# Filler matmuls into a free PSUM bank, a later planned end for TensorE's results, and a new order, in a planned one-core kernel

## The chip, the cores and the metric

The kernel runs on one core of a Trainium2 chip. The metric is the device time of one execution in microseconds (us); the time of the kernel before is the median of 3 runs. Engines go by these names: PE or TensorE (matmuls), DVE or VectorE, ACT or ScalarE, POOL or GpSimd, SP or SyncE, on whose queue all DMAs of this kernel are issued.

## What is computed

The reference is a sliding-window attention (half of the heads with a plain window of 32 tokens, half with a dilated one of 32 tokens in steps of 4), whose output feeds a first MLP (softmax-gated, with a layer norm) and a second one (softplus).

```python
# q, k, v: (4, 8, 576, 64); scores masked per head, softmax, times v
x = attn_out.transpose(0, 2, 1, 3).reshape(2304, 512)
h = x @ w_in                                   # 512 -> 1024
e = exp(h - max(h)); solu = h * e / (sum(e) + 1e-9)
y = (solu - mean) / sqrt(var + 1e-6) * g_ln @ w_out   # 1024 -> 512
h2 = y @ w2_in                                 # 512 -> 2048
out = softplus(h2) @ w2_out                    # 2048 -> 512, (2304, 512)
```

## The kernel before

Nearly every product is computed in three matmuls of fp16 halves: each operand is split into a high half and a low half (high by high, high by low, low by high). So each weight block is loaded in fp64, converted to fp32 by three VectorE instructions (`to_f32`, L768), squared and summed on ScalarE for its scale, and split into the two halves (`weights`, L791). There are 48 such blocks: 8 of w_in, 8 of w_out, and four quarters of the second MLP with 4 + 4 blocks each (`w2_quarter`, L887).

The attention is done in 28 pairs of blocks. The first 10 run in fp32 (`pair32` and `block32`, L1040 and L1081), because their inputs' scales aren't known yet: TensorE transposes q and k into a bank, computes scores, transposes the exponentials and multiplies by v; the result is transposed into columns of a bank and copied into a ring `xr`, the high half by ScalarE or VectorE (L631 or L667, the helpers), the low half by VectorE (L643). The other 18 pairs run in fp16 halves with DMA transposes (`block`, L1184). The first MLP takes 18 tiles of 128 tokens (`m1`, L1287), its second matmul and the second MLP 9 groups of 256 tokens (`y_stage`, L1390, and `mlp2`, L1437).

PSUM has eight banks of 512 fp32 columns here: `banks[0]` to `banks[3]`, shared by the attention and by the outputs of y_stage and mlp2 (several pools with one flag `taken` per bank, L611 and L612), and two double banks `ps_w` for the wide results.

Nothing is issued in the order in which it is written. Each step is an `Op` with its possible engines and costs, its predecessors and its buffers. `Plan.order` (L148) then plays the execution through in Python: a clock, one ready list per engine sorted by due time (`TABLE`, one number in tenths of a microsecond for each of the 2524 steps), the costs `act_cost`, `dve_cost`, `pe_cost` (L280: duration, and time until others see the result) and `moving` (L288: a DMA's time on the queues). A buffer is free in the plan when the last user has ended there. The resulting order is emitted engine by engine and kept; the engines then run it in order and wait for each other with semaphores.

Where TensorE has nothing ready in the plan before 400 us, a filler of `FILL` = 0.24 us is planned (L261 to L265: `None` in the order). The emission (L1581 and after) turns it into a 512-column matmul of `eye` into the first `ps_w` as long as no step has used `ps_w`, and after that into eight matmuls of 60 columns into columns 452 to 511 of bank 1 (L1590), which no step reads. Bank 1 also holds attention results and small sums in its other columns.

Lines that the rows name: L631 ScalarE activation, L635 and L637 VectorE tensor-scalar, L640 VectorE scalar-tensor-tensor, L643 VectorE tensor-tensor, L646 reciprocal, L649 matmul, L655 TensorE transpose.

Of the kernel before, what the change touches and what calls it, by code (L numbers as in the profile page):

```python
# [24 lines left out]
class Pool:  # L25
# [8 lines left out]
    def add(self, t, until=10 ** 9, since=0, opens=(), place=None):  # L34


        self.slots.append([t, until, since, list(opens), [False] if place is None else place])
# [28 lines left out]
class Plan:  # L66
# [8 lines left out]
    FILL = (0.24, 0.48)  # L75
# [9 lines left out]
    def __init__(self, due, table):  # L85
        self.ops = []
        self.due, self.table = due, table

# [59 lines left out]
    def order(self):  # L148
# [25 lines left out]
        while events:  # L174
            now = heapq.heappop(events)
            while ends and ends[0][0] <= now + 1e-9:
                _, i, elsewhere = heapq.heappop(ends)
                o = self.ops[i]
                if elsewhere:
                    over.add(o)  # L180
                    for b in o.uses:
                        b.left -= 1
                        if b.left == 0:
                            b.slot[4][0] = False
                for s in o.succ:
                    for e in s.opts:
                        if (e != o.on) == elsewhere:
                            s.wait[e] -= 1
                            if not s.wait[e] and s.on is None:
                                bisect.insort(ready[e], (s.late + self.shy(s, e), s.i))  # L190
# [70 lines left out]
            if idle_at["PE"] <= now + 1e-9 and now < self.FILL_END:  # L261
# [3 lines left out]
                out.append(None)  # L265
# [14 lines left out]
def pe_cost(us):  # L280
    return {"PE": (us, 0.12)}
# [6 lines left out]
def moving(packets, size, lag=2.2):  # L288

    return 1.07 * packets * (12 + size / 21.0) / 16000, lag  # L290
# [3 lines left out]
def kernel(  # L294
# [1332 lines left out]
```

## Time and profile before

| | us |
|---|---|
| median of 3 runs | 722.39 (720.72 to 723.04) |
| profiled execution, own time | 724.25 |
| its span, first to last instruction | 722.40 |
| TensorE busy in the span | 695.0 (96%) |
| VectorE busy | 510.1 (71%) |
| ScalarE busy | 460.1 (64%) |

The profile counts an engine's busy time by instruction; a filler counts as busy like any matmul. A row with "x968" is a group of 968 instructions, then their busy time in us and the mean ns of one, from its start to its modelled end, so that matmuls that follow each other overlap. Behind it stands the idle time of the engine just before them, and what ended it ("<-"). "Waits" rows read: who waited, for whom, us in total, times, the longest. PEclk is the granted clock of TensorE as a share of 2.4 GHz.

### The profile page before, as it was taken

How to read it: one execution, taken by the hardware profiler on the slowest of the kernel's cores; microseconds unless marked ns; L12 is line 12 of the kernel's file. 1: busy time of each engine (PE TensorE's matmuls, PEld its weight loads, DVE VectorE, ACT ScalarE, POOL GpSimd, SP SyncE). 2: the span in 40 equal slices, each digit the busy share in tenths (PEclk: the TensorE clock that was granted, in tenths of full speed). 3: DMA queues.
4: the chain of work that ended last, by engine and by line, in shares of the span. 5: the costliest groups of instructions: out<-in, count | busy, mean ns of one | idle time of the engine just before them, and what ended most of it. 6: DMA issues, size and time to landing. Idle time of an engine off the chain costs nothing.

```text
span 722.4 us, 15990 instructions
## 1 busy us (share of the span) xinstructions
PE 695.0 (96%) x6186; PEld 494.3 (68%) x6186; DVE 510.1 (71%) x1550; ACT 460.1 (64%) x938; POOL 3.5 (0%) x22
## 2 busy tenths in 40 slices
PE   6789889999999999999999999999999999999997
PEld 3566777868766577777665866776686567778573
DVE  4899889999999894966889578489857662310411
ACT  4687788698999486777785489268756552321121
POOL 1000000000000000000000000000000000000000
PEclk9879999999999999999999999999999999999999
DMA  9987866767875446976775185465614111100100
GB/s 250 297 216 216 232 155 155 173 147 159 188 181 143 127 135 171 233 129 156 154 127 111 45 179 128 74 110 127 127 37 74 41 30 27 33 1 1 59 1 29
DMA packets 186779, 89.91 MB, mean 124 GB/s; under 512 B 157000, under 2 KB 174416, under 8 KB 186704
## 3 DMA queue, kind: packets, MB, share of 16 engines
q1 hardware_dynamic: 186704, 88.90, 52.5%
q8 instruction: 48, 0.79, 0.5%
q14 instruction: 27, 0.22, 0.1%
HBM read 54.53 MB, written 4.72 MB: 82 GB/s over the span
## 4 chain that ended last, share of the span: by engine, by line
PE 77%; DVE 13%; DMA 5%; ACT 4%; issue 1%; SPq 0%; DVEq 0%; ACTq 0%
PE bank L649 39%; PE ps_w L649 32%; PE bank L1590 3%; DVE W L640 3%; DMA E<-in_moe_w_in_dram 2%; DMA W<-in_v_dram 1%; PE bank L655 1%; DVE E L640 1%; ACT xr L631 1%; DMA kT<-qk 1%; ACT E L631 1%; DVE xr L643 1%; ACT xf L631 1%; DMA xd<-x 1%; DVE s L1202 1%
## 5 line engine op out<-in xcount | busy, mean ns | idle before, releaser
L649 PEld LDWEIGHTS <-W 128*128 128x128 f16 x2592 | 252.0, 98 | 35.8 <-issue 0.4
L649 PE MATMUL bank<-y,W 128*128 128x256 f16 x1728 | 197.9, 273 | 0.3 <-DVE y L640 0.3
L649 PE MATMUL ps_w<-W,g 128*128 128x512 f16 x864 | 195.0, 379 | 0.0
L649 PEld LDWEIGHTS <-g 128*128 128x128 f16 x864 | 83.5, 98 | 90.9
L649 PE MATMUL ps_w<-W,xr 128*128 128x512 f16 x432 | 97.9, 379 | 0.0
L649 PE MATMUL bank<-lnT,W 128*128 128x256 f16 x864 | 97.4, 273 | 0.0
L631 ACT ACTIVATE r<-bank,invC 128x512 f32<-128x512 f32 x72 | 49.2, 685 | 71.9 <-PE bank L649 63.8
L640 DVE SCALAR_TENSOR_TENSOR g<-r,KR,g 128x512 f16<-128x512 f32 x72 | 53.6, 745 | 51.7 <-ACT g L631 48.9
L1595 ACT ACT_TABLE_LOAD x59 | 75.7, 1283 | 1.1
L649 PEld LDWEIGHTS <-xr 128*128 128x128 f16 x432 | 41.6, 99 | 44.9 <-issue 0.2
L631 ACT ACTIVATE s<-s 96x128 f32<-96x128 f32 (+3 forms) x144 | 43.7, 375 | 15.9 <-DVE s L637 15.7
L631 ACT ACTIVATE E<-E 128x768 f32<-128x768 f32 (+3 forms) x53 | 38.8, 733 | 9.7 <-DVE E L640 5.9
L1202 DVE CUSTOM_DVE_ANT_0 s<-bank,band,bsc 96x128 f32<-96x128 f32 (+3 forms) x144 | 39.0, 324 | 4.3 <-PE bank L649 3.7
L1590 PE MATMUL bank<-eye 128*128 128x60 bf16 x968 | 34.2, 191 | 7.7 <-DVE xr L643 2.5
L1590 PEld LDWEIGHTS <-eye 128*128 128x128 bf16 x968 | 31.9, 98 | 9.9 <-issue 9.4
L635 DVE TENSOR_SCALAR g<-r,KR 128x512 f16<-128x512 f32 x29 | 13.9, 478 | 35.1 <-PE ps_w L649 30.6
L640 DVE SCALAR_TENSOR_TENSOR y<-bank,y 128x512 f16<-128x512 f32 x18 | 12.3, 685 | 33.8 <-ACT y L631 33.8
L631 ACT ACTIVATE y<-bank 128x512 f16<-128x512 f32 x18 | 10.7, 592 | 37.7 <-PE bank L649 37.6
L631 ACT ACTIVATE g<-r,KR 128x512 f16<-128x512 f32 x43 | 30.8, 720 | 5.1 <-PE ps_w L649 4.2
L631 ACT ACTIVATE hl<-e,st 128x1024 f16<-128x1024 f32 x18 | 22.2, 1235 | 15.9 <-DVE st L640 9.7
L631 ACT ACTIVATE xf<-bank,rs 80x64 f32<-80x64 f32 (+1 forms) x104 | 23.6, 305 | 11.4 <-DVE rs L646 8.6
L631 ACT ACTIVATE e<-ps_w,st,bsc 128x1024 f32<-128x1024 f32 x16 | 19.3, 1204 | 13.8 <-DVE st L635 6.7
(190 smaller groups left out, 891.2 us busy)
## 6 DMA issues: line engine op xcount, KB each, us to landing
E<-in_moe_w_in_dram SPq DMA_DIRECT2D x19, 512.0 KB, 5.4
E<-in_moe_w_out_dram SPq DMA_DIRECT2D x16, 512.0 KB, 4.2
out_dram<-osb SPq DMA_DIRECT2D x18, 256.0 KB, 2.1
W<-in_moe_w_out_dram SPq DMA_DIRECT2D x8, 512.0 KB, 4.7
E<-in_q_dram SPq DMA_DIRECT2D x9, 384.0 KB, 3.4
E<-in_k_dram SPq DMA_DIRECT2D x9, 384.0 KB, 3.4
E<-in_v_dram SPq DMA_DIRECT2D x9, 384.0 KB, 3.3
W<-in_moe_w_in_dram SPq DMA_DIRECT2D x5, 512.0 KB, 8.9
```

What stands on the lines that cost most here:

```text
L631: pin(nc.scalar.activation(out=out, in_=in_, func=func, **kw))
L635: pin(nc.vector.tensor_scalar(out=out, in0=in0, scalar1=s1, scalar2=None, op0=op0))
L640: pin(nc.vector.scalar_tensor_tensor(out=out, in0=in0, scalar=s, in1=in1, op0=op0, op1=op1, **kw))
L643: pin(nc.vector.tensor_tensor(out=out, in0=a, in1=b, op=op))
L649: pin(nc.tensor.matmul(out, l, r, start=start, stop=stop))
L655: pin(nc.tensor.transpose(out, in_, eye32[:in_.shape[0], :in_.shape[0]]))
L1202: pin(nc.vector.tensor_tensor_reduce(out=sv()[:rows, h, :nk], in0=sb.t[:rows, h, :nk], in1=band[:rows, 48 - m:48 - m + nk], scale=sc[:rows ...
L1590: pin(nc.tensor.matmul(banks[1][:, 452:512], eye, eye[:, 0:60], start=False, stop=False, skip_group_check=True))
L1595: pin(nc.scalar.preload_act_table_set(TABLES[tab]))
```

## The change

Three things change.

- A filler goes into a bank that is free in the plan at that moment, the one that has been free longest: each bank's flag now holds the time at which it came free, `fills` lists the four banks and the first half of both `ps_w`, and the order holds the chosen bank in place of `None`. If none is free, `None` stays in the order and nothing is emitted, though the plan still counts the filler. It is always one matmul of 512 columns; the eight small ones, and the one before them, are gone. `FILL` goes from 0.24 to 0.235 us.
- The plan's numbers: a TensorE result is seen by others 0.26 us after its matmul (0.2 for long ones) where it was 0.12; a DMA takes 1.05 in place of 1.07 times its formula and 2.05 in place of 2.2 us of lag, unless a call names its own lag.
- `TABLE`, the due times of all steps, is replaced as a whole, so that the order is another.

```diff
-        self.slots.append([t, until, since, list(opens), [False] if place is None else place])
+        self.slots.append([t, until, since, list(opens), [False, 0.0] if place is None else place])
...
-    FILL = (0.24, 0.48)
+    FILL = (0.235, 0.48)
...
+        self.fills = []
...
                         if b.left == 0:
-                            b.slot[4][0] = False
+                            b.slot[4][:] = [False, now]
...
-                out.append(None)
+                free = [f for f in self.fills if not f[0][0]]
+                out.append(min(free, key=lambda f: f[0][1])[1] if free else None)
...
 def pe_cost(us):
-    return {"PE": (us, 0.12)}
+    return {"PE": (us, 0.26 if us < 2 else 0.2)}
...
-def moving(packets, size, lag=2.2):
+def moving(packets, size, lag=2.05):
 
-    return 1.07 * packets * (12 + size / 21.0) / 16000, lag
+    return 1.05 * packets * (12 + size / 21.0) / 16000, lag
...
     TABLE = (
-        132, 520, 330, 83, 561, 140, 146, 157, 191, 249, 235, 436, 342, 89, 150, 150, 164, 172, -3353, 168,
...
-    taken = [[False] for _ in banks]
+    taken = [[False, 0.0] for _ in banks]
...
+    P.fills = [*zip(taken, banks), *((x[4], x[0][:, 0]) for x in ps_w.slots)]
     order = P.order()
-    tab, unused = 1, True
-    mm(banks[1][:, 452:512], eye, eye[:, 0:60], True, True)
+    tab = 1
     for o in order:
         if o is None:
-            if unused:
-                mm(ps_w.slots[0][0][:, 0], eye, eye.unsqueeze(1).broadcast_to([128, 4, 128]), True, True)
-                continue
-            for _ in range(8):
-                pin(nc.tensor.matmul(banks[1][:, 452:512], eye, eye[:, 0:60], start=False, stop=False, skip_group_check=True))
             continue
-        unused = unused and not any(b.pool is ps_w for b in o.uses)
+        if not isinstance(o, Op):
+            mm(o, eye, eye.unsqueeze(1).broadcast_to([128, 4, 128]), True, True)
+            continue
```

## Rows read from the trace of the kernel before

**Rows 1.** The page, busy time of each engine over the span.

```profile
PE 695.0 (96%) x6186; PEld 494.3 (68%) x6186; DVE 510.1 (71%) x1550; ACT 460.1 (64%) x938; POOL 3.5 (0%) x22
```

**Rows 2.** Busy time by stretch: length, engines, granted clock, DMA share, GB/s.

```profile
core 0: us, PE busy (x) PEld busy (x) DVE busy (x) ACT busy (x) POOL busy (x), PEclk, DMA share, GB/s
0.00:40.00 40.00, 30.41 (x201) 20.20 (x201) 26.80 (x73) 23.27 (x68) 3.52 (x22) 0.83 1.00 270
40.00:160.00 120.00, 109.73 (x1532) 84.25 (x1531) 109.79 (x317) 96.11 (x257) 0.00 (x0) 0.97 0.71 184
160.00:255.00 95.00, 92.84 (x829) 64.58 (x828) 92.31 (x278) 79.68 (x168) 0.00 (x0) 1.00 0.67 160
255.00:718.00 463.00, 461.98 (x3630) 325.28 (x3627) 280.49 (x886) 260.35 (x447) 0.00 (x0) 1.00 0.42 89
```

**Rows 3.** The fillers of L1590 alone, by stretch: length, PE and PEld busy, clock, DMA.

```profile
40.00:160.00 120.00, 30.12 (x848) 28.06 (x848) 0.97 0.71 184
160.00:255.00 95.00, 4.11 (x120) 3.81 (x120) 1.00 0.67 160
sum 722.40, PE 34.23 PEld 31.87; mean PE 6.85 PEld 6.37
```

**Rows 4.** TensorE's groups of instructions, shapes apart: fillers, and a matmul of 512 columns.

```profile
L649 PE MATMUL ps_w<-W,g 128*128 128x512 f16 x864 | 195.0, 379 | 0.0
...
L1590 PE MATMUL bank<-eye 128*128 128x60 bf16 x968 | 34.2, 191 | 7.7 <-DVE xr L643 2.5 <-ACT xf L631 2.3 <-ACT xr L631 1.7
L649 PE MATMUL ps_w<-eye 128*128 128x512 bf16 x40 | 14.1, 469 | 0.0
```

**Rows 5.** Timeline of 103 to 111 us: start us, us, instruction, idle before it.

```profile
103.82 0.33 ACT L631 ACTIVATE xr<-bank 128x192 f16<-128x192 f32 x1 [0.37 <-PE bank L1590]
...
104.21 0.38 PE L1590 MATMUL bank<-eye 128*128 128x60 bf16 x8 [0.42 <-ACT xr L631]
...
105.20 0.36 DVE L643 TENSOR_TENSOR xr<-bank,xr 128x192 f16<-128x192 f32 x1 [1.31 <-PE bank L1590]
```

**Rows 6.** VectorE's waits from 40 to 160 us.

```profile
DVE xr L643 <- PE bank L1590: 4.1, 5, 1.3
DVE tmp L819 <- PE bank L1590: 1.6, 3, 0.6
DVE xr L643 <- ACT xf L631: 0.9, 1, 0.9
DVE rs L637 <- PE bank L649: 0.9, 2, 0.7
DVE rs L637 <- ACT xf L631: 0.7, 1, 0.7
DVE pT L667 <- PE bank L655: 0.3, 1, 0.3
DVE W L637 <- DMA E<-in_moe_w_in_dram: 0.3, 1, 0.3
...
DVE rs L637 <- PE bank L1590: 0.2, 1, 0.2
```

**Rows 7.** ScalarE's waits for TensorE from 40 to 160 us.

```profile
ACT xr L631 <- PE bank L655: 3.8, 3, 1.5
...
ACT xr L631 <- PE bank L1590: 1.9, 3, 1.1
...
ACT qT L631 <- PE bank L649: 1.3, 1, 1.3
...
ACT xf L631 <- PE bank L1590: 0.5, 1, 0.5
```

**Rows 8.** TensorE's timeline from 84 us, ten groups of eight fillers in a row.

```profile
84.35 2.36 PE L1590 MATMUL bank<-eye 128*128 128x60 bf16 x80 [0.58 <-ACT xr L631]
```

**Rows 9.** The chain of work, 40 to 130 us: start us, us, what.

```profile
92.33 2.59 PE ps_w L649 x12
```

**Rows 10.** The page's DMA issues: count, KB each, median us to landing.

```profile
E<-in_moe_w_in_dram SPq DMA_DIRECT2D x19, 512.0 KB, 5.4
```

286 rows, old and new, of the table TABLE are left out of this document.

## The prediction

> **What bounds the kernel now.** I read the page's busy shares first. TensorE is busy 96% of the span [rows 1], which invites the conclusion that only fewer matmuls could help. The table by stretch and the rows of the fillers correct that. From 255 to 718 us TensorE is idle for 463.00 - 461.98 = 1.0 us, without a filler: a solid block of work that no order can shorten, and behind it lie 4.4 us for the last copy and its store. Before 255 us it is idle for 9.6, 10.3 and 2.2 us in the three stretches [rows 2], and 34.2 us of its "busy" time are fillers of 60 columns at L1590 [rows 3], 14.1 us more the early fillers of 512 columns [rows 4]. So 22.1 + 48.3 = 70 us of the span are TensorE waiting for others. The rest is work that stays. The span falls only if the block starts earlier, hence only if whoever feeds TensorE before 255 us gets faster.
>
> Who feeds it? From 40 to 160 us VectorE is busy 109.8 of 120 us, ScalarE 96.1; from 160 to 255 us VectorE 92.3 of 95 us, ScalarE 79.7 [rows 2]. VectorE converts the weights, writes the low halves into the ring xr and takes the maxima, so VectorE's lost time sets the pace until TensorE is saturated. In 40 to 160 us it lost 10.2 us.
>
> **Where VectorE loses it.** The timeline at 104 us shows the mechanism. ScalarE writes the high half of xr out of a bank (103.82 to 104.15). The next filler starts only at 104.21, after 0.42 us of idling, and names ScalarE's xr as its releaser. VectorE's xr, which reads the same bank after ScalarE, starts at 105.20, after 1.31 us of waiting for a filler [rows 5]. Fillers and readers both use bank 1 and take turns, although the filler's columns 452 to 511 are never read. From 40 to 160 us VectorE waits for fillers 4.1 + 1.6 + 0.2 = 5.9 us [rows 6] and ScalarE 1.9 + 0.5 = 2.4 us [rows 7]; TensorE idles 7.7 us ahead of fillers in the whole execution [rows 4].
>
> **The change part by part.**
>
> *Fillers into a free bank.* A group of eight 60-column matmuls becomes one of 512 columns. Ten groups in a row took 2.36 us [rows 8], 0.236 us a group; twelve 512-column matmuls of the real work took 2.59 us [rows 9], 0.216 each. For 121 groups that is 2.4 us less of filler, which costs or brings nothing: fillers stand where TensorE has nothing else. A real matmul can now be late by at most one 0.216 us filler, before by a group of 0.236. What does count is the bank. The new filler takes the one that has been free longest by the plan, so each reader of the old contents has finished by the plan, and a later reader waits only for the real matmul between. VectorE's 5.9 us go. I take all of them as gain, because VectorE has no slack there that could have covered them. ScalarE's 2.4 us I take as nothing: its 24 us of idle time there cover them; without the cover they would be the further end, 8.3 us. The lower end is nothing, if other waits step in. The fillers' own 7.7 us I also put at nothing, hidden behind VectorE.
>
> Which wait is a bank's and which an address's? The rows show two operations on different columns of one bank waiting for each other. The Trainium skill, "PSUM — Partial Sum Buffer", section "PSUM bank collisions raise a hardware error", asks that accesses be guarded by bank and quadrant, not by address, which agrees with that row; by its rule a whole-bank filler in a bank that is still being read would also wait, which is the rival "not free" below.
>
> *TensorE's results planned later.* The plan allowed 0.12 us from a matmul's slot to its consumer, now 0.26 or 0.20. A 512-column matmul's mean row is 0.379 us [rows 4] for a 0.216 us slot, so 0.16 us pass before its end: 0.12 was too little, and engines that work in order were given consumers of TensorE that weren't ready. What that costs now: VectorE waits for real matmuls 0.9 + 0.3 = 1.2 us in 40 to 160 us [rows 6], ScalarE 3.8 + 1.3 = 5.1 us [rows 7]. I take VectorE's whole and a quarter of ScalarE's, since it has 24 us idle: 1.2 + 1.3 = 2.5 us. Ends: 0 and 6.3 us.
>
> *Loads planned earlier.* 1.07 to 1.05 and 2.2 to 2.05 us put a load's planned arrival earlier by 0.15 us and 2% of the queue's backlog: 0.15 + 0.02 x 40 = at most 0.95 us after the first 40 us, where the DMA share is 1.00 [rows 2]. VectorE waits for loads 0.3 us in 40 to 160 us [rows 6], so there is spare time: nothing taken, the other end is the slower rival.
>
> *The order made anew.* Nearly all of the table's 2524 due times are new; what each moves on the queues can't be read from the profile of before. Bounds: the one stretch with TensorE dry behind a saturated VectorE is 160 to 255 us, 2.2 us idle and 4.1 us of fillers [rows 2, 3], so 6.3 us could go; for a loss I take the same size. I take 0, because VectorE, nearly full there, leaves an order little to win. Each step of the work still runs once, on the same queues, with the same 48 weight blocks to load.
>
> *The first matmul of 60 columns* goes away: one filler less while VectorE still waits for its first weights; nothing.
>
> **Sum.** 5.9 + 2.5 = 8.4 us. The profiled execution took 724.25 us, 722.40 of them the span and 1.85 around it, which I leave. That run lies 1.86 us above the median of 722.39 us, so I take the 8.4 us off the median: **714.0 us**. With its own ends this case spans 709 (most of what ScalarE waits for fillers and late matmuls, 2.4 and the other 3.8 us, is gained as well: 5 us more) to 719 (the replanning gives nothing, and the order loses 2.5).
>
> **The rivals.**
>
> *The dry stretch closes too* (0.20): the 6.3 us of 160 to 255 us go as well, 722.4 - 8.4 - 6.3 = 707.7 us. For it: with VectorE 8 us ahead, the last quarter's weights are ready when TensorE's stock runs out. Against: VectorE is as full there as before.
>
> *VectorE's time is given back* (0.14): after 160 us TensorE and VectorE are both above 97% [rows 2], and a VectorE that is ahead meets other waits, such as ScalarE's share of the same chains (xf, 0.9 + 0.7 us [rows 6]). Then about 1 us stays, 721.4 us. Against it: that stretch has no wait of any size on VectorE today.
>
> *The banks aren't free* (0.07): the change doesn't do what it says, if on the chip the readers lag behind the plan and fillers still wait. The 5.9 us stay lost and the 2.5 come, 719.9 us. Against: the bank is the longest free.
>
> *VectorE stuck behind a load* (0.10, slower): VectorE works in order; if a conversion is put ahead of its load's arrival, everything behind it waits. The place is 20 to 160 us, with the 40 blocks after the first eight, each landing some 5.4 us after its issue [rows 10]. The price is up to 0.95 us each by the sum above; the point is (8.4 + 2.2)/40 = 0.27 us per block, from which the run is slower than before. At 0.4 us each: 714 + 16 = 730 us. For it: the DMA share of 1.00 early. Against: 0.3 us of such waits in 40 to 160 us.
>
> *A clock that falls* (0.03): where no bank is free by the plan, nothing is emitted, where before a filler always was. The granted clock was 0.83 in 0 to 40 us and 0.97 in 40 to 160 us with 30.1 us of small fillers [rows 2, 3]. At 0.83 the 109.7 - 30.1 = 79.6 us of real work there would take 79.6 x 0.97/0.83 = 93.0 us, 13.4 more, against 40 us of idle time and fillers. Half hidden: 714 + 6.7 = 720.7 us. The Trainium skill, "TensorE: Matmul & The Clock Gate", section "Why this matters for your kernels", warns of idle gaps between matmul bursts, after which the clock is halved; that speaks against leaving fillers out.
>
> **How the numbers follow.** 0.46 is left for the forecast. 0.3%, about what a measurement here tells from no change, is 2.2 us. Faster: 0.46 + 0.20 + 0.03 of the given-back case + 0.04 of the banks + 0.01 of the clock = 0.74. Same: 0.09 + 0.03 + 0.02 = 0.14. Slower: 0.02 + 0.10 = 0.12. The range 706 to 722 leaves out the load rival (0.10), half of the given-back case (0.07) and a little below the dry-stretch rival (0.03).
>
> **What would show it.** Right: no VectorE or ScalarE wait names the filler's line, VectorE's idle time in 40 to 160 us falls from 10.2 to about 4 us, fillers are of 512 columns and spread over several banks, TensorE's solid block starts some 8 us earlier and lasts as long, and the clock there is still near 0.97. Wrong: waits of TensorE's fillers for readers of their bank remain; VectorE waits for weight loads after 20 us; or the block starts earlier but has holes after 255 us, where each microsecond idle counts in full.

## The result and the profile after

The kernel after takes **714.1 us** (median of 4 runs, 713.2 to 715.53) where before takes 722.12 us in the same comparison (4 runs, 720.72 to 723.04): a ratio of 0.9892, 95% interval 0.9869 to 0.9916. That is 8.0 us less. The profiled execution took 715.53 us, the slowest of its four.

The page of the kernel after, its span and busy shares, which answer to [rows 1]:

```profile
span 713.8 us, 14287 instructions
...
PE 690.8 (97%) x5334; PEld 475.8 (67%) x5334; DVE 505.4 (71%) x1548; ACT 453.7 (64%) x913; POOL 3.5 (0%) x22
```

Busy time by stretch in the kernel after (length, PE, PEld, DVE, ACT, POOL with counts, granted clock, DMA share, GB/s), which answers to [rows 2]:

```profile
0.00:40.00 40.00, 34.11 (x244) 20.39 (x245) 27.06 (x70) 21.44 (x64) 3.52 (x22) 0.96 1.01 271
40.00:160.00 120.00, 110.70 (x815) 74.48 (x814) 115.09 (x336) 105.32 (x279) 0.00 (x0) 0.91 0.71 188
160.00:255.00 95.00, 93.12 (x717) 62.12 (x715) 91.31 (x286) 78.70 (x165) 0.00 (x0) 1.00 0.73 162
255.00:709.40 454.40, 452.84 (x3564) 318.82 (x3563) 271.20 (x859) 247.81 (x408) 0.00 (x0) 1.00 0.42 89
```

VectorE now loses 120 - 115.09 = 4.9 us from 40 to 160 us, before 10.2. Its waits there, which answer to [rows 6] (who, for whom: us, times, longest):

```profile
DVE xr L644 <- ACT xr L632: 1.6, 2, 1.3
DVE s L1094 <- PE bank L650: 1.6, 1, 1.6
DVE E L638 <- DMA W<-in_moe_w_out_dram: 1.0, 1, 1.0
DVE hl L644 <- ACT hl L632: 0.3, 1, 0.3
```

A filler and a real matmul now share line L650, so the one wait for TensorE needs a second look: `s` reads the bank in which scores were just computed, 1.6 us. The order of after with the old fillers, whose late ones have a line of their own, has the same wait of 1.6 us, and there it names the real matmuls' line. The waits of `xr` and `tmp` for TensorE that made up 5.7 of the 5.9 us in [rows 6] are gone. TensorE's fillers, which answer to [rows 3, 4]:

```profile
L650 PE MATMUL ps_w<-eye 128*128 128x512 bf16 x91 | 24.8, 392 | 0.6 <-DVE e L641 0.6
L650 PE MATMUL bank<-eye 128*128 128x512 bf16 x66 | 19.4, 423 | 4.0 <-POOL eye L709 4.0
```

There are 157 fillers of 512 columns, spread over single and double banks. The plan has 191: for 34 of the 76 that come after the first use of `ps_w` it finds no free bank, and nothing is emitted. Ahead of them TensorE idles 4.6 us, 4.0 of them before `eye` exists at the start. The 0.6 us that are left stand against the 7.7 us ahead of the small fillers before.

Where the 8 us went is a sum over TensorE, whose real work is the same in both kernels (695.0 - 48.3 = 646.7 and 690.8 - 44.2 = 646.6 us). Its time without real work (fillers, plus span minus busy) was 48.3 + (722.4 - 695.0) = 75.7 us before and is 44.2 + (713.8 - 690.8) = 67.2 us after. The difference of 8.5 us is the difference of the two spans, 8.6.

### The profile page after: what moved, and what is told of

Read it like the earlier page. It is cut to its first block, busy times and chain, and to the rows that moved or that the text cites. A ratio compares the mean times of both kernels' runs of the same rounds, so it can differ in the third digit from the quotient of the medians.

```text
span 713.8 us, 14287 instructions
## 1 busy us (share of the span) xinstructions
PE 690.8 (97%) x5334; PEld 475.8 (67%) x5334; DVE 505.4 (71%) x1548; ACT 453.7 (64%) x913; POOL 3.5 (0%) x22
## 4 chain that ended last, share of the span: by engine, by line
PE 70%; DVE 14%; DMA 8%; ACT 4%; issue 3%; SPq 0%; ACTq 0%; DVEq 0%
PE bank L650 38%; PE ps_w L650 30%; DVE W L641 2%; DMA pT<-p 2%; DMA E<-in_v_dram 1%; PE bank L656 1%; DMA rq<-in_q_dram 1%; DVE E L641 1%; DVE s L1203 1%; DVE e L641 1%; DMA W<-in_moe_w_out_dram 1%; DMA xr<-x 1%; DMA qT<-qk 1%; DMA xd<-in_v_dram 1%; DVE p L644 1%
## 5 line engine op out<-in xcount | busy, mean ns | idle before, releaser
L650 PEld LDWEIGHTS <-W 128*128 128x128 f16 x2592 | 252.2, 98 | 37.1 <-issue 2.0
L650 PE MATMUL bank<-y,W 128*128 128x256 f16 x1728 | 196.7, 273 | 1.0 <-ACT r L632 1.0
L650 PE MATMUL ps_w<-W,g 128*128 128x512 f16 x864 | 194.9, 379 | 1.0 <-DVE osb L641 1.0
L650 PEld LDWEIGHTS <-g 128*128 128x128 f16 x864 | 83.4, 98 | 92.6 <-issue 1.3
L650 PE MATMUL ps_w<-W,xr 128*128 128x512 f16 x432 | 99.7, 385 | 0.1
L650 PE MATMUL bank<-lnT,W 128*128 128x256 f16 x864 | 98.3, 273 | 0.3 <-DMA lnT<-hl 0.3
L650 PEld LDWEIGHTS <-xr 128*128 128x128 f16 x432 | 42.3, 100 | 48.1 <-issue 3.0
L632 ACT ACTIVATE E<-E 128x768 f32<-128x768 f32 (+3 forms) x56 | 40.4, 726 | 10.6 <-DMA E<-in_v_dram 3.2
L636 DVE TENSOR_SCALAR g<-r,KR 128x512 f16<-128x512 f32 x34 | 16.4, 482 | 37.1 <-PE ps_w L650 35.7
L632 ACT ACTIVATE y<-bank 128x512 f16<-128x512 f32 x15 | 8.9, 594 | 41.5 <-PE bank L650 41.5
L632 ACT ACTIVATE g<-r,KR 128x512 f16<-128x512 f32 x38 | 27.3, 719 | 5.5 <-PE ps_w L650 4.8
L650 PEld LDWEIGHTS <-eye 128*128 128x128 bf16 (+2 forms) x177 | 17.4, 106 | 19.6 <-issue 5.3
L1329 DVE TENSOR_REDUCE st<-ps_w 128x1 f32<-128x1024 f32 x18 | 21.9, 1216 | 7.0 <-PE ps_w L650 7.0
L641 DVE SCALAR_TENSOR_TENSOR E<-E 128x512 int32<-128x512 int32 x40 | 26.1, 683 | 0.0
```

Of the source, the lines that this page charges most:

```text
L632: pin(nc.scalar.activation(out=out, in_=in_, func=func, **kw))
L636: pin(nc.vector.tensor_scalar(out=out, in0=in0, scalar1=s1, scalar2=None, op0=op0))
L641: pin(nc.vector.scalar_tensor_tensor(out=out, in0=in0, scalar=s, in1=in1, op0=op0, op1=op1, **kw))
L650: pin(nc.tensor.matmul(out, l, r, start=start, stop=stop))
L1329: ({"DVE": (1.142, 0.14)}, lambda e: pin(nc.vector.tensor_reduce(out=col(0), in_=ph(), axis=AXX, op=ALU.max, negate=True)), [mb], [ps]),
```

## The experiments

Each kernel was timed against before on its own chip. Before's median was 722.59 us beside the fillers alone, the order alone, the early results and the old order with early fillers alone; 722.31 beside the small fillers in a free bank, the new order without late fillers and without any, and the first run with the bank freed last; 722.87 beside the other four. A difference between two kernels that ran on different chips is taken here from what each lost or won against its own before. "Old order" is that of before with its costs and table, "new order" that of after. The two crossed cases, the new table with all the old costs or the old table with all the new ones, give no complete order (the plan runs into a point where nothing can start), so they weren't tried. Medians in us, with the ratio to before and its interval:

| fillers | old order | new order |
|---|---|---|
| none | 724.29, 1.0015 (1.0000 to 1.0031) | 720.78, 0.9973 (0.9953 to 0.9993) |
| early ones alone | 722.4, 1.0001 (0.9987 to 1.0014) | 714.64, 0.9890 (0.9866 to 0.9914) |
| early, then 8 x 60 columns in bank 1 | before | 714.84, 0.9890 (0.9867 to 0.9913) |
| early, then 8 x 60 columns in a free bank | 716.1, 0.9907 (0.9883 to 0.9932) | not run |
| 512 columns, bank free longest | 714.9, 0.9887 (0.9870 to 0.9905) | after: 714.1, again 714.39, 0.9883 (0.9863 to 0.9902) |
| 512 columns, bank freed last | 715.23, 0.9903 (0.9883 to 0.9924) | 711.22, 0.9838 (0.9812 to 0.9864); again 710.96, 0.9842 (0.9821 to 0.9863) |

"Early" are those before a step uses `ps_w`: 40 in the old order, 115 in the new one.

**The fillers alone, in the old order.** Before, with the change's lists of free banks and its emission, but before's table, costs and `FILL`:

```diff
-                out.append(None)
+                free = [f for f in self.fills if not f[0][0]]
+                out.append(min(free, key=lambda f: f[0][1])[1] if free else None)
...
-            for _ in range(8):
-                pin(nc.tensor.matmul(banks[1][:, 452:512], eye, eye[:, 0:60], start=False, stop=False, skip_group_check=True))
...
+        if not isinstance(o, Op):
+            mm(o, eye, eye.unsqueeze(1).broadcast_to([128, 4, 128]), True, True)
+            continue
```

> The order of before, unchanged; only the fillers go, one matmul of 512 columns each, into the bank that the plan of before knows to be free. Bank theory: the 5.9 us that VectorE waited for fillers from 40 to 160 us go, and the time falls to about 716 us (714 to 718), ratio 0.992; no wait names a filler. Order theory: the fillers' waits only stood in place of other waits, the gain came from the new order, and this kernel takes 720 to 723 us, with VectorE's idle time from 40 to 160 us still near 10 us.

Measured: 714.9 us, 7.7 less than before. The same steps in the same order on each engine, and VectorE is busy 116.08 of 120 us. Its stretch from 40 to 160 us, then its longest waits there:

```profile
40.00:160.00 120.00, 113.34 (x842) 74.40 (x841) 116.08 (x330) 102.82 (x270) 0.00 (x0) 0.96 0.72 189
```

```profile
DVE s L1095 <- PE bank L651: 1.0, 1, 1.0
DVE tmp L821 <- PE bank L651: 0.9, 1, 0.9
DVE st L1330 <- PE ps_w L651: 0.4, 1, 0.4
DVE xr L645 <- ACT xr L633: 0.3, 1, 0.3
```

VectorE's idle time fell by 116.08 - 109.79 = 6.3 us, a little over the 5.9 of [rows 6]; no wait of `xr` for TensorE is left. Step by step against before, VectorE is level or up to 2 us behind until about 75 us, 4.2 us ahead at 111 us, 7.0 at 150 us, 6.5 at 200 us, 9.3 at its end (the profiled execution of before lies 1.9 us above its median, so part of the 9.3 is its own). So the lead is not given back. Of the 161 fillers that the plan has, 149 stand in this trace; for 12 it finds no free bank.

**The order alone, with the old fillers.** After, with before's fillers:

```diff
-                free = [f for f in self.fills if not f[0][0]]
-                out.append(min(free, key=lambda f: f[0][1])[1] if free else None)
+                out.append(None)
...
+            for _ in range(8):
+                pin(nc.tensor.matmul(banks[1][:, 452:512], eye, eye[:, 0:60], start=False, stop=False, skip_group_check=True))
```

> The order of the changed kernel with the fillers of before (eight of 60 columns in bank 1, and 512 columns in the first double bank until that is first used). Bank theory: VectorE waits some 5 us for fillers again, and the time rises from 714.1 to 718 to 721 us. Order theory: 714 to 715 us, no change from the changed kernel.

Measured: 714.84 us, as much as the fillers alone brought. The parts give 7.7 and 7.8 us, and together 8.0. They don't add: VectorE's idle time from 40 to 160 us falls from 10.2 us to 3.9 with the fillers alone, 4.5 with the order alone and 4.9 with both. The stretch, then TensorE's groups, whose late fillers still sit in bank 1:

```profile
40.00:160.00 120.00, 115.34 (x1323) 84.86 (x1323) 115.47 (x335) 105.32 (x276) 0.00 (x0) 0.96 0.69 189
```

```profile
L649 PE MATMUL ps_w<-eye 128*128 128x512 bf16 x115 | 32.2, 403 | 0.0
L1590 PE MATMUL bank<-eye 128*128 128x60 bf16 x608 | 21.1, 191 | 1.9 <-ACT xr L631 1.0 <-ACT xf L631 0.4 <-DVE rs L637 0.3
```

There are 608 / 8 = 76 groups in bank 1 where [rows 4] have 968 / 8 = 121, TensorE idles 1.9 us ahead of them instead of 7.7, and VectorE's waits for them in 40 to 160 us have one row:

```profile
DVE rs L637 <- PE bank L1590: 0.5, 1, 0.5
```

In the old order of instructions 40 late fillers stand between the high and the low half of a write of `xr`, in the new one 10. More of the filling (115 early ones where 40 were) happens while `ps_w` is still unused. So the new order's late fillers hold up little; where its gain comes from is told by the runs without them, below.

**Bank or size?** The fillers of the first experiment, but eight of 60 columns in place of one of 512 once `ps_w` is in use:

```diff
-    tab = 1
+    tab, unused = 1, True
...
-            mm(o, eye, eye.unsqueeze(1).broadcast_to([128, 4, 128]), True, True)
+            if unused:
+                mm(o, eye, eye.unsqueeze(1).broadcast_to([128, 4, 128]), True, True)
+                continue
+            for i in range(8):
+                pin(nc.tensor.matmul(o[:, 452:512], eye, eye[:, 0:60], start=i == 0, stop=True, skip_group_check=True))
             continue
+        unused = unused and not any(b.pool is ps_w for b in o.uses)
```

> The order of before; fillers go into the bank that the plan knows to be free, but the later ones stay eight matmuls of 60 columns each (columns 452 to 511 of that bank). If the bank is what counts, the time is that of the 512-column fillers in the free bank: 714 to 717 us, and no wait names a filler. If the size counts (one instruction for eight, fewer weight loads, shorter wait of real work behind a filler), it stays at 719 to 723 us.

Measured: 716.1 us, its interval overlapping that of the 512-column ones. It is the bank: against its own before this kernel wins 6.2 us, where the 512-column fillers won 7.7. The 1.5 us between them, which the intervals can't tell from nothing, are left for the size. Here the small fillers have a line of their own, L1594. TensorE idled before none of them, and no wait of VectorE or ScalarE before 260 us names that line:

```profile
L1594 PE MATMUL ps_w<-eye 128*128 128x60 bf16 x752 | 25.1, 191 | 0.0
...
L1594 PE MATMUL bank<-eye 128*128 128x60 bf16 x120 | 3.8, 190 | 0.0
```

**The late fillers taken away, old order.** Before without the loop of eight:

```diff
-            for _ in range(8):
-                pin(nc.tensor.matmul(banks[1][:, 452:512], eye, eye[:, 0:60], start=False, stop=False, skip_group_check=True))
```

> The kernel before without the eight-matmul fillers; the early ones of 512 columns stay. Bank theory: as with the free bank, VectorE's 5.9 us of waits for fillers go, but the clock is no longer held up in 60 to 160 us. If the clock hardly matters there because TensorE waits for VectorE anyway, 716 to 718 us; if the clock counts, the granted clock falls from 0.97 to about 0.8 from 40 to 160 us, and the time is 720 to 730 us.

Measured: 722.4 us, the same as before. Its stretch from 40 to 160 us and VectorE's longest waits in it:

```profile
40.00:160.00 120.00, 101.80 (x710) 68.78 (x711) 111.09 (x319) 97.68 (x257) 0.00 (x0) 0.84 0.70 183
```

```profile
DVE xr L667 <- PE bank L655: 1.6, 1, 1.6
DVE s L1093 <- PE bank L649: 1.4, 3, 0.6
DVE pT L667 <- PE bank L655: 1.3, 1, 1.3
DVE tmp L757 <- PE bank L649: 1.2, 1, 1.2
```

The waits for fillers are gone, and waits for real matmuls stand in their place: the granted clock there is 0.84, against 0.97 in [rows 2]. VectorE still loses 8.9 us. So before's 121 late groups were worth nothing net: what they held up in clock they took in waits. In a free bank the fillers (109 late ones) do only the first, 722.4 - 714.9 = 7.5 us.

**The same cuts in the new order, and no fillers at all.** First, after, whose fillers stop when a step uses `ps_w`:

```diff
-    tab = 1
+    tab, unused = 1, True
...
-            mm(o, eye, eye.unsqueeze(1).broadcast_to([128, 4, 128]), True, True)
+            if unused:
+                mm(o, eye, eye.unsqueeze(1).broadcast_to([128, 4, 128]), True, True)
             continue
+        unused = unused and not any(b.pool is ps_w for b in o.uses)
```

> The changed kernel without the fillers that come after the first use of a double bank; the early ones stay. If fillers pay by the clock also in the new order, as the old order without small fillers suggests (722.4 us with no filler to wait for), the granted clock from 40 to 160 us falls well below 0.91 and the time rises by 4 to 9 us, to 718 to 723 us. If the new order has little use for fillers, it stays at 714 to 716 us; that would also explain why the old fillers cost it nothing.

Then both orders without fillers: after's, and the first experiment's for the old order, each with this edit:

```diff
         if not isinstance(o, Op):
-            mm(o, eye, eye.unsqueeze(1).broadcast_to([128, 4, 128]), True, True)
             continue
```

> The changed kernel without any filler. If the early fillers, which hold the clock from 0 to 60 us, pay too, it is slower than the one without late fillers by some 2 to 8 us: 718 to 730 us. If VectorE sets the pace there whatever the clock, the same as without late fillers.

> The order of before without any filler. With the new order without any filler at 720.8 us, the difference is what the order alone is worth. If the order has a worth of its own of some 8 us, as with the old fillers, this takes 727 to 732 us. If its gain lay in where and how many fillers it places, 720 to 723 us.

Measured: 714.64, 720.78 and 724.29 us. The stretch from 40 to 160 us of the three, in that order:

```profile
40.00:160.00 120.00, 105.17 (x780) 72.16 (x779) 114.95 (x335) 104.97 (x276) 0.00 (x0) 0.90 0.69 189
```

```profile
40.00:160.00 120.00, 100.61 (x712) 70.65 (x711) 110.44 (x322) 98.75 (x269) 0.00 (x0) 0.82 0.69 182
```

```profile
40.00:160.00 120.00, 101.19 (x685) 68.90 (x684) 109.88 (x318) 96.21 (x259) 0.00 (x0) 0.83 0.72 184
```

In the new order the early fillers bring 720.78 - 714.64 = 6.1 us and the late ones nothing that can be told; the clock is 0.90 without the late ones and 0.91 with them. In the old order it is the other way round: the late ones in a free bank bring 7.5 us (0.84 to 0.96), the 40 early ones 1.6 (clock 0.83 and 0.84; 724.29 is 1.4 above its before, 722.4 is 0.2 below), and the intervals of those two kernels overlap. In these runs fillers pay where they raise the clock of that stretch and VectorE's idle time falls with it. The order by itself, without fillers, is worth 3.0 us (1.4 above its before in the old order, 1.5 below in the new one).

The two kernels with early fillers alone have no late filler that a reader could wait for, and the new order is still ahead, 7.7 us below its before against 0.2: 7.5 us. Of these 3.0 are the order's own, and 4.5 go with 115 early fillers in place of 40 (6.1 - 1.6). So the new order's gain with the old fillers does not come from turn-taking that it avoids. It comes without late fillers as well; the order only places them so that they cost little.

**Results planned early again.** After with the old time from a matmul to its consumer. The due times stay those made for 0.26 and 0.2:

```diff
-    return {"PE": (us, 0.26 if us < 2 else 0.2)}
+    return {"PE": (us, 0.12)}
```

> The changed kernel with TensorE's results planned at 0.12 us after their matmul, as before; the new due times and the new fillers stay, so the plan makes another order from the same due times. If the 0.26 and 0.20 us are worth what they save in waits for results that come later than planned, 2 to 3 us are lost: 716 to 718 us. If due times and costs only work as a pair that was searched for together, the order falls apart much further: over 722 us. If neither matters: 714 us.

Measured: 725.76 us, 1.0035 (1.0016 to 1.0055): 11.7 us over after, 3.2 us slower than before. But this is no measure of the term, because it changes the order as well, and the due times don't fit it. VectorE loses no more from 40 to 160 us (115.09 us busy); what is lost shows behind it, where ScalarE is busy 70.92 us in place of 78.70:

```profile
160.00:255.00 95.00, 93.12 (x692) 60.16 (x691) 91.08 (x278) 70.92 (x145) 0.00 (x0) 1.00 0.66 150
```

TensorE is as busy there as in after, but more of it is fillers. Its matmuls with `eye`, behind 160 us fillers only (length, busy, clock, DMA share, GB/s):

```profile
160.00:255.00 95.00, 9.13 (x37) 1.00 0.66 150
255.00:400.00 145.00, 4.26 (x19) 1.00 0.68 151
```

That is 13.4 us, where after has 2.4 us before 255 us and none behind it.

**The bank that was freed last.** If the plan's "free" were wrong on the chip, the bank freed last would bring the waits back. After, and the first experiment for the old order, with one word changed; and after once more, for its spread:

```diff
-                out.append(min(free, key=lambda f: f[0][1])[1] if free else None)
+                out.append(max(free, key=lambda f: f[0][1])[1] if free else None)
```

> The changed kernel with the filler in the bank that came free last by the plan, where it was the one that has been free longest. If the plan's free banks are free on the chip only because of that margin, fillers wait for readers again and the time rises by 2 to 6 us, to 716 to 720 us. If the plan is true to the chip within a few tenths of a microsecond, 714 to 715 us.

> The changed kernel once more, beside the one with the newest free bank. If that one is really faster, this takes 713 to 715 us again; if its 711.2 us were those of another chip, this takes about 711 us too.

> The changed kernel with fillers in the bank that came free last, once more. Really faster: 710 to 712 us, 2 to 4 us less than the changed kernel in the same job. A chip's difference: the same as the changed kernel.

> The order of before, 512-column fillers in the free bank that came free last by the plan. If the choice among the free banks matters by itself, this gains as in the new order, 2 to 4 us: 711 to 713 us. If the old order's plan, which takes TensorE's results 0.12 us after the matmul, is too early for a bank just freed, fillers wait for readers and it takes 716 to 720 us. If the choice doesn't matter: 715 us.

Measured: in the old order 715.23 us, the same as with the bank free longest (714.9). In the new order 711.22 and 710.96 us, below 714.1 and 714.39 for after, and each of its nine executions (709.72 to 712.29) lies below each of after's nine (712.51 to 715.53): this version **beats both kernels**, by 3.4 us against after in the last comparison. Its fillers do wait for others, but little: some 1.1 us in either order, without the 4.0 us for `eye` at the start. In the old order these waits are all ahead of one group:

```profile
L651 PE MATMUL bank<-eye 128*128 128x512 bf16 x73 | 20.2, 391 | 1.1 <-DVE xr L645 0.4 <-ACT xf L633 0.4 <-ACT kT L633 0.2
```

VectorE's instructions come in the same order with either bank. The profiled executions of the last comparison lie only 1.7 us apart (712.51, the fastest of its five, and 710.78), so they can show half of the difference at most. From 220 to 232 us the repeat of after stalls, here its row and then that of the version with the bank freed last:

```profile
220.00:232.00 12.00, 11.10 (x63) 5.35 (x62) 10.97 (x26) 8.16 (x18) 0.00 (x0) 1.00 0.68 132
```

```profile
220.00:232.00 12.00, 11.97 (x67) 5.74 (x66) 12.00 (x27) 8.93 (x18) 0.00 (x0) 1.00 0.73 129
```

VectorE loses 1.0 us there, because it waits for a ScalarE instruction that came after 3.26 us without a visible cause; in the first profile of after it came after 3.36 (timeline of the repeat of after, then of the other; start, us, instruction, idle before it):

```profile
225.88 0.63 ACT L632 ACTIVATE p<-s 96x512 f16<-96x512 f32 x1 [3.26 <-issue]
...
226.54 0.69 DVE L644 TENSOR_TENSOR p<-s,p 96x512 f16<-96x512 f32 x1 [1.03 <-ACT p L632]
```

```profile
224.18 0.63 ACT L632 ACTIVATE p<-s 96x512 f16<-96x512 f32 x1 [1.80 <-issue]
```

That can't be the whole cause: the version without late fillers has the short wait too (1.77 us) and takes 714.64 us. Why the other bank is 3.4 us faster in the new order, and not in the old one, **stays open**.

## Why the prediction was right, and which of its steps were not

The total came out: 714.0 us predicted, 714.1 measured, the 8.4 us taken off against 8.0. The split did not, so that the total is this close is partly luck.

**What bounds the kernel: right.** TensorE's 75.7 us without real work was the only place to gain, and the gain is what it lost there. Every version that gained in the stretch where VectorE feeds TensorE has VectorE idle less from 40 to 160 us: 10.2 us before, 3.9 with the fillers alone, 4.5 with the order alone, 4.9 after. Early results are the exception: as little idle time (4.9), and the loss behind 160 us.

**Fillers into a free bank: right in mechanism, too small in size.** 5.9 us were taken, 7.7 came. VectorE's idle time accounts for 6.3 of them in 40 to 160 us; its lead in the profiled executions grows from 7.0 us at 150 us to 9.3. The lower end, nothing because other waits step in, came true where the late fillers were merely taken away. The step that put "ScalarE's 2.4 us" and "the fillers' own 7.7 us" at nothing is where the rest could come from; no run splits it. The measured value lies within the ends that were given, 0 to 8.3.

**Size counts for nothing: borne out** within 1.5 us, by the small fillers in a free bank.

**Results planned later, 2.5 us, and the order made anew, 0: the step that failed.** Alone, with the old fillers, the new costs and order bring 7.8 us; with early fillers alone 7.5; without fillers 3.0; on top of fillers in a free bank 0.3 to 0.8, which the intervals can't tell from nothing. The sum added two ways of shortening the same idle time of VectorE as if they were two losses. Its two errors, 1.8 us too little and some 1.9 too much, cancelled. What the prediction missed is that an order also sets where the fillers stand: the new one puts 115 in place of 40 ahead of the first use of `ps_w`, the clock from 40 to 160 us is 0.90 without any late filler, and the late ones are then worth nothing that can be told (3.4 us in the bank freed last, for a cause that is open). No run splits the order's own 3.0 us into their parts. The price of 0.12 against 0.26 us alone remains untried, since the costs only make an order together with their table, and so do the loads' new numbers, which the prediction put at nothing.

**Fillers cost or bring nothing: half right.** For their length it holds (the size, above). But they also hold the clock, and VectorE waits for late real matmuls without them: 7.5 us in the old order. The Trainium skill, "TensorE: Matmul & The Clock Gate", section "Why this matters for your kernels", warns of idle gaps between bursts; the cut of the late fillers agrees (clock 0.97 to 0.84), but the trace adds that a filler which others wait for can cost all that it holds.

**The solid block starts 8 us earlier and lasts as long: wrong in form.** TensorE's last filler starts at 229.3 us, before at 253.3. The block after it is longer, about 479.7 us in place of 464.5, and has 2.7 us of holes where it had 1.0; 1.6 of them lie behind 255 us, which the prediction names as a sign of being wrong, but they are only 0.5 us more than before's. What counted was the sum of the time without real work.

**The rivals.** *Banks not free*: refuted; TensorE idles 0.6 us ahead of its fillers for other engines where it was 7.7, and even with the bank freed last some 1.1 us. *Time given back*: refuted by the lead that stays. *Dry stretch closes too*: only in part; in 160 to 255 us VectorE idles 3.7 us (2.7 before), TensorE 1.9 (2.2 before), its fillers take 2.4 us (4.1 before), and the time is 6.4 us above that rival's 707.7. *VectorE behind a load*: one wait of 1.0 us, no cascade. *A clock that falls*: its condition came true, 34 late fillers found no bank, and the clock fell from 0.97 to 0.91. The price was nothing that can be told: the same order with all its fillers emitted, in bank 1, has 0.96 and takes 714.84 us. The kernel after in steps of four microseconds:

```profile
80.00:84.00 4.00, 0.68 (x4) 0.52 (x5) 4.00 (x14) 4.00 (x12) 0.00 (x0) 0.83 0.94 292
84.00:88.00 4.00, 3.03 (x17) 2.36 (x16) 4.00 (x10) 3.97 (x13) 0.00 (x0) 0.50 0.58 187
88.00:92.00 4.00, 3.86 (x22) 3.42 (x22) 4.00 (x14) 3.75 (x9) 0.00 (x0) 0.50 0.77 200
92.00:96.00 4.00, 4.00 (x11) 1.36 (x10) 4.00 (x16) 4.00 (x11) 0.00 (x0) 0.50 0.93 216
96.00:100.00 4.00, 3.26 (x32) 1.98 (x31) 3.71 (x14) 3.61 (x9) 0.00 (x0) 0.97 0.61 161
```

TensorE was idle for 3.3 of 4 us, and after that the clock stood at its lower level, 1.2 GHz, from 84 to 96 us. In the 16 us from 80 to 96 us VectorE was busy without a gap, so the low clock delayed nobody there who sets the pace.

## What to carry to other kernels

Give a matmul that exists only to hold the clock a PSUM bank which nobody is reading or about to read: columns that nobody reads in a bank that others use still make readers and fillers take turns (by semaphores of the program; no run shows what would happen without them). Read a filler's worth from two runs, one without it and one with it elsewhere; a run without it alone said "worth nothing" here, and hid 7.5 us of clock and as much of waits. Don't add up two parts of a change that shorten the same engine's idle time in the same stretch: run each alone, and run each without what you think it saves, as the new order without late fillers.

## What the runs showed that was not expected

The choice among free banks matters in one order (711.0 against 714.4 us) and not in the other (715.2 and 714.9), with the same number of fillers (157 in the new order, 149 in the old one). The cause isn't known.

A clock of 0.82 to 0.84 from 40 to 160 us goes with VectorE idle for 8.9 to 10.1 us, one of 0.90 with 5.0; but 0.97 went with 10.2 in before. Clock alone doesn't tell the time of this stretch: who waits does.
